# Block attention feeding a token and channel MLP, one core: the first batch in a hand-set order, its values transposed on TensorE, its queries transposed in fp32, and another layout of the DRAM scratch

## Chip, cores and metric

One Trainium2 chip (trn2), one core. Times are device microseconds (us) of whole executions. "Span" is the length of one profiled execution; the named engines are PE (TensorE), DVE (VectorE), ACT (ScalarE), POOL (GpSimd) and SP, which here only issues DMAs. The "granted clock" is the TensorE clock that the throttle let through, as a share of full speed. A run is marked slow when it is over 1.5% above the fastest of the same kernel, and fast otherwise; all comparisons below are of fast runs unless it says otherwise.

## The reference, cut to what matters

```python
# 4 batches, 8 heads, 768 positions of 64, 8 blocks of 96 positions
P = sort_net                                    # 8x8 for each batch and head
for _ in range(5):                              # Sinkhorn
    P = exp(P - max(P)); P = P / rowsum(P); P = P / colsum(P)
k_sorted = einsum('bhij,bhjcd->bhicd', P, k_blocks)     # blocks of keys mixed
v_sorted = einsum('bhij,bhjcd->bhicd', P, v_blocks)     # blocks of values mixed
attn = softmax(q_block @ k_sorted_block.T / 8)          # within each block
x = attn @ v_sorted_block                               # -> (batch, 768, 512)
u = x + lam * (w_tok @ (alpha1 * x + beta1))            # token mixing
out = u + lam * (relu((alpha2 * u + beta2) @ w_ch1) @ w_ch2)   # channel MLP, 512 -> 2048 -> 512
```

## The kernel before: the parts that matter here

Batches are software-pipelined: the attention of batch b is traced ahead of the channel MLP of batch b-1, and a scheduler orders the instructions of each engine. For batch 0 nothing lies before it, so its loads, Sinkhorn, attention and token mixing are a stage of their own. The mixed values come out of the matmul with (head, block) on the partitions, but the attention's product needs the position within a block there. They are regrouped through a scratch tensor in DRAM:

```python
vscr = dram.tile([B, BLK, H * NB, GRP], F16)        # GRP = 66: 64 values, a one for the softmax sum, one of padding
def mix_v(b):
    for n in range(6):
        nc.tensor.matmul(vps, bigV[b], raw[:, n * 512:(n + 1) * 512])
        ...                                          # copied to vA[:, 48, 0:64], vA[:, :, 64:66] = 1
    for th in range(2):                              # write: pieces of 66 float16 = 132 bytes
        nc.sync.dma_start(vscr[b, th * HB:(th + 1) * HB].rearrange("t c d -> c t d"), vA[th * 64:(th + 1) * 64])
    for par in range(2):                             # read: 8.4 KB per partition in one piece
        nc.sync.dma_start(Vs[b % 2][par * HB:(par + 1) * HB],
                          vscr[b].rearrange("(tt par) c d -> par tt c d", par=2)[par])
# ... cut ...
def emit_q(b):      # queries cast to float16 on DVE, 24 transposes on PE, 8 copies on DVE
def prep_wtok():    # w_tok (768x768) turned on PE: 36 transposes of 96 columns, 36 of 32
def prep_affine():  # alpha1*lam, beta1*lam on POOL; six row sums of w_tok on DVE
def prep_w2():      # W2 = W2 * lam on POOL, 16 instructions
def moe_a(b):       # token mixing (tok_ps): u = x + lam*(...), u transposed into a2T
# ... cut ...
mix_v(0); mix_k(0); cast_q(0); emit_q(0); emit_attention(0)
prep_wtok(); prep_affine(); moe_a(0); prep_w2()
for b in range(1, B):
    load_q(b); cast_q(b); ...; mix_v(b); mix_k(b); emit_q(b); emit_attention(b)
    moe_h(b - 1, 0); moe_ch(b - 1, 0); moe_h(b - 1, 1); moe_a(b); moe_ch(b - 1, 1)
```

The softmax here doesn't subtract the row's maximum and nothing guards it: scores larger than these inputs give would overflow.

## Time and profile before

| | before |
|---|---|
| median of the first three runs | 349.29 us (348.66 to 352.27) |
| first product of batch 0 (x_ps) | 70.1 us |
| first token mixing (tok_ps) of batches 0, 1, 2, 3 | 82.0, 145.1, 212.6, 280.4 us |
| PE idle between 47.5 and 70 us | all of it |

From the page's part 2, the span of 348.4 us in 40 equal slices: tenths of busy time for PE, of the granted TensorE clock, and of the 16 DMA engines:

```profile
PE   0358940099777996999959999999599988999995
...
PEclk9975555557999998999998999999899999999999
DMA  7999999931995996019851220597302100201102
```

PE has a hole in slices 7 and 8, the clock stands at 0.5 from slice 4 to 9, and the DMA engines are full from slice 2 to 8. The chain of waits (start, duration, what) says what the hole waited for:

```profile
6.13 25.41 DMA b2col<-in_moe_beta_dram
31.55 0.02 issue
31.56 32.53 DMA vscr<-vA
...
64.53 5.51 DMA Vs_224<-vscr
...
70.08 1.62 PE x_ps L322 x16
...
86.23 17.98 DMA vscr<-vA
...
104.65 5.76 DMA Vs_225<-vscr
```

The write of batch 0's values into the scratch takes 32.5 us of that chain and the read back 5.5; batch 1's write takes 18 and its read 5.8. The page's list of DMA issues (KB each, median us from issue to landing):

```profile
vscr<-vA SPq DMA_DIRECT2D x8, 396.0 KB, 18.1
...
Vs_224<-vscr SPq DMA_DIRECT2D x4, 396.0 KB, 4.8
Vs_225<-vscr SPq DMA_DIRECT2D x4, 396.0 KB, 4.7
```

Each batch has two of these writes, issued together: the same bytes land in 18 us when they are written in 132-byte pieces and in under 5 when they are read in large ones.

Last, two stretches of the first stage (length, then busy time of PE, weight loads, DVE, ACT and POOL with instructions, granted clock, DMA share, GB/s):

```profile
28.00:47.50 19.50, 19.41 (x85) 10.49 (x83) 10.03 (x11) 6.24 (x12) 4.92 (x6) 0.50 1.24 188
47.50:70.00 22.50, 0.00 (x0) 0.00 (x0) 1.12 (x2) 0.75 (x1) 5.59 (x4) 0.50 1.16 167
```

PE works through the transposes of w_tok without a gap and then stops for 22.5 us.

### The profile page before, as it was taken

What the parts mean: (1) busy time and instruction counts of PE and PEld (TensorE: products, weight loads), DVE (VectorE), ACT (ScalarE), POOL (GpSimd) and SP (SyncE); (2) the same over time, 40 slices, a digit from 0 to 9 for tenths busy, and PEclk for the clock granted to TensorE, in tenths of its full rate; (3) what the DMA queues carried; (4) which work ended last, traced back from release to release, by engine and by line L of the source; (5) the groups of instructions that cost most, each with busy time, mean ns of one, the idle gap of its engine ahead of it and who ended that gap; (6) DMA issues with size and microseconds to landing.
All of it is one profiled execution on the core that took longest, in us unless ns stands there. A gap on an engine that the chain in (4) does not pass through costs nothing.

```text
span 348.4 us, 4808 instructions
## 1 busy us (share of the span) xinstructions
PE 281.4 (81%) x1801; PEld 161.7 (46%) x1812; DVE 178.9 (51%) x398; ACT 143.5 (41%) x304; POOL 105.5 (30%) x98
## 2 busy tenths in 40 slices
PE   0358940099777996999959999999599988999995
PEld 0144520084445643554647454546464644454552
DVE  7899300169997822197757603959471046101001
ACT  2252310042597502566446055646450644170620
POOL 6216050006999966001300850031027300000000
PEclk9975555557999998999998999999899999999999
DMA  7999999931995996019851220597302100201102
GB/s 177 243 251 200 183 182 132 185 113 50 66 28 101 215 216 196 2 20 56 50 155 46 78 60 0 34 55 85 106 2 60 31 3 0 81 11 54 38 27 63
DMA packets 41367, 31.85 MB, mean 91 GB/s; under 512 B 27520, under 2 KB 36480, under 8 KB 40960
## 3 DMA queue, kind: packets, MB, share of 16 engines
q1 hardware_dynamic: 35040, 19.88, 39.7%
q0 software_dynamic: 6304, 11.67, 18.1%
q8 instruction: 14, 0.23, 0.3%
q14 instruction: 9, 0.07, 0.1%
HBM read 33.67 MB, written 9.54 MB: 124 GB/s over the span
## 4 chain that ended last, share of the span: by engine, by line
PE 52%; DMA 31%; DVE 10%; SPq 3%; ACT 2%; issue 1%; DVEq 0%
PE ch_ps L451 21%; PE h_ps L439 20%; DMA vscr<-vA 14%; DMA b2col<-in_moe_beta_dram 7%; PE x_ps L322 5%; DMA qf<-in_q_dram 3%; DMA Vs_224<-vscr 3%; DMA Vs_225<-vscr 3%; PE sc_ps L305 3%; PE tok_ps L399 2%; DVE toktmp L404 2%; PE uT_ps L412 1%; DVE qbd_216 L291 1%; DVE ost L456 1%; DVE x_347 L352 1%
## 5 line engine op out<-in xcount | busy, mean ns | idle before, releaser
L443 ACT ACTIVATE hTa<-h_ps 128x384 bf16<-128x384 f32 x96 | 47.0, 492 | 69.0 <-PE h_ps L439 68.4
L439 PEld LDWEIGHTS <-W1p 128*128 128x128 bf16 x512 | 50.3, 101 | 33.3 <-issue 6.5
L451 PE MATMUL ch_ps<-W2p,hTa 128*128 128x512 bf16 x277 | 65.3, 379 | 0.4
L312 ACT ACTIVATE et<-sc_ps 96x384 f16<-96x384 f32 x64 | 27.8, 489 | 46.3 <-PE x_ps L322 34.5
L451 PEld LDWEIGHTS <-hTa 128*128 128x128 bf16 x288 | 27.9, 98 | 32.0
L322 PEld LDWEIGHTS <-et 96*96 96x96 f16 x256 | 19.8, 149 | 36.0 <-DMA Vs_224<-vscr 26.9
L404 DVE TENSOR_TENSOR toktmp<-tok_ps,a1lB 128x512 f32<-128x512 f32 x24 | 16.4, 686 | 35.4 <-PE tok_ps L399 35.3
L322 PE MATMUL x_ps<-Vs_224,et 96*96 96x65 f16 x128 | 11.3, 240 | 26.3 <-DMA Vs_224<-vscr 26.3
L113 DVE CAST qn<-qf 128x768 f16<-128x768 f32 x14 | 9.4, 683 | 35.5 <-DMA qf<-in_q_dram 35.5
L451 PE MATMUL ch_ps<-W2p,hTb 128*128 128x512 bf16 x96 | 24.6, 379 | 0.2
L272 ACT CAST kT<-k_ps 64x256 f16<-64x256 f32 x48 | 17.6, 368 | 16.9 <-PE q_ps L283 11.4
L380 POOL TENSOR_TENSOR W2p<-W2p,lamB 128x512 bf16<-128x512 bf16 x16 | 18.5, 1197 | 12.4 <-DMA W2p<-in_moe_w_ch_dram 12.4
L399 PEld LDWEIGHTS <-w_tokT 128*128 128x128 f16 x144 | 13.9, 98 | 16.2 <-issue 1.7
L270 DVE CAST kT<-k_ps 64x256 f16<-64x256 f32 x48 | 19.9, 415 | 0.8
L329 DVE RECIPROCAL recip<-x_ps 96x4 f32<-96x4 f32 x64 | 9.6, 169 | 20.8 <-PE x_ps L322 20.0
L305 PEld LDWEIGHTS <-kT 128*96 128x96 f16 x128 | 16.0, 148 | 7.6 <-issue 3.1
L443 ACT ACTIVATE hTb<-h_ps 128x384 bf16<-128x384 f32 x32 | 15.7, 490 | 6.0 <-PE h_ps L439 5.5
L439 PE MATMUL h_ps<-a2T_659,W1p 128*128 128x384 bf16 x64 | 14.7, 326 | 0.8 <-DVE a2T_660 L424 0.8
L439 PE MATMUL h_ps<-a2T_660,W1p 128*128 128x384 bf16 x64 | 12.4, 358 | 3.4 <-DVE ost L456 3.4
L451 PEld LDWEIGHTS <-hTb 128*128 128x128 bf16 x96 | 9.4, 98 | 11.3
L439 PE MATMUL h_ps<-a2T_1402,W1p 128*128 128x384 bf16 x64 | 14.4, 337 | 0.0
L322 PE MATMUL x_ps<-Vs_225,et 96*96 96x65 f16 x128 | 9.6, 214 | 5.8 <-DMA Vs_225<-vscr 5.8
(247 smaller groups left out, 462.9 us busy)
## 6 DMA issues: line engine op xcount, KB each, us to landing
qf<-in_q_dram SPq DMA_DIRECT2D x14, 384.0 KB, 5.7
out_dram<-ost SPq DMA_DIRECT2D x24, 192.0 KB, 2.2
vscr<-vA SPq DMA_DIRECT2D x8, 396.0 KB, 18.1
W1p<-in_moe_w_ch_dram POOLq DMA_DIRECT2D x4, 512.0 KB, 21.1
W2p<-in_moe_w_ch_dram POOLq DMA_DIRECT2D x4, 512.0 KB, 23.2
Vs_224<-vscr SPq DMA_DIRECT2D x4, 396.0 KB, 4.8
Vs_225<-vscr SPq DMA_DIRECT2D x4, 396.0 KB, 4.7
out_dram<-ost SPq DMA_DIRECT2D x24, 64.0 KB, 2.0
```

The source lines that it names most:

```text
L270: nc.vector.tensor_copy(dst, src)
L272: nc.scalar.copy(dst, src)
L305: nc.tensor.matmul(sps[:, ii, :, :].rearrange("p a t -> p (a t)"), kT[:, h4 * NB + 2 * g + ii, :], qb[:, 2 * g + ii, :, :].rearrange("p a ...
L312: nc.scalar.activation(et[:], sps[:], AF.Exp, scale=scale)
L322: nc.tensor.matmul(xps[:, ii * 2 + h2, 0:D + 1], ets[g][:, ii, h2, :], Vs[b % NV][:, col, 0:D + 1], start=True, stop=True,)
L329: nc.vector.reciprocal(recip[:], xps[:, :, D])
L380: nc.gpsimd.tensor_tensor(W2p[:, m, :], W2p[:, m, :], lamB[:], ALU.mult)
L399: nc.tensor.matmul(tps[:], w_tokT[:, ks, kt * 128:(kt + 1) * 128], x128[:, ks, :], start=(ks == 0), stop=(ks == NT - 1),)
L404: nc.vector.tensor_tensor(tmp[:], tps[:], a1lB[:], ALU.mult)
L439: nc.tensor.matmul(hps[:], W1p[:, ci, m * 128:(m + 1) * 128], a2T_of[b][hf][:, ci, :], start=(ci == 0), stop=(ci == CT - 1),)
L443: nc.scalar.activation(hT[m], hps[:], AF.Relu)
L451: nc.tensor.matmul(cps[:], hT[m][:, kk * 128:(kk + 1) * 128], W2p[:, m, :], start=(m == 0), stop=(m == HT - 1),)
```

## The change

The intent: keep batch 0's values off the loaded DMA queues, by mixing them the way the keys are mixed and transposing them on PE; transpose its queries straight from fp32, without a cast on DVE; write all of the first stage in the order in which each engine shall run it; and lay out the scratch, which batches 1 to 3 still use, the other way round. The diff, cut to its core:

```diff
+    class Engine:                       # wraps each engine; while fixed, instructions keep their program order
+        fixed = True
+        ...
+                if Engine.fixed:
+                    tc.keep_in_program_order(ins)
-    vscr = dram.tile([B, BLK, H * NB, GRP], F16, name="vscr", tag="vscr")
+    vscr = dram.tile([B, H, NB, BLK, D], F16, name="vscr", tag="vscr")
     # write: now 6 KB per partition in one piece; the ones stay in Vs
-                vscr[b, th * HB:(th + 1) * HB, :, :].rearrange("t c d -> c t d"),
+                vscr[b, :, :, th * HB:(th + 1) * HB, :].rearrange("h i t d -> (h i) t d"),
     # read: now 64 float16 = 128 bytes in one piece
-                Vs[b % NV][par * HB:(par + 1) * HB, :, :],
-                vscr[b].rearrange("(tt par) c d -> par tt c d", par=2)[par],
+                Vs[b % NV][par * HB:(par + 1) * HB, :, 0:D],
+                vscr[b].rearrange("h i (tt par) d -> par tt (h i) d", par=2)[par],
+    def q_first(n):                      # 16 calls, put between the Sinkhorn steps and the mixing of the values
+        for kk in range(3):
+            pe.transpose(qps[:, kk, :], qn_of[0][1][h4][:, h2, 3 * kh + kk, :], ident32[:])   # fp32
+        act.copy(...)
+    def turn_v(b, vT):                   # 32 transposes of 96 columns, 4 copies on DVE
     ...
-        nc.vector.tensor_reduce(rs[:, kt:kt + 1], wt16[:, kt, :], AXX, ALU.add)
+    def prep_rs():                       # the row sums as 36 matmuls with a column of ones
-    mix_v(0)
-    mix_k(0)
-    ...
+    mixing_matrices(0)
+    for g in range(6):
+        vT0 = mix_t(0, 1, share=(4, 4, 3, 2, 1, 1), into=vT0, groups=range(g, g + 1))
+        for n in range(9 + 2 * g, min(11 + 2 * g, 16)):
+            q_first(n)
+    mix_k(0, ps=psb, share=(0,) * 6, groups=range(3))
+    turn_v(0, vT0)
+    mix_k(0, ps=psb, share=(2,) * 6, into=kT_of[0], groups=range(3, 6))
+    ...
+    emit_attention(0, between)           # three of the six parts of w_tok between the scores
+    prep_rs()
+    mix_v(1, alone=True)
+    Engine.fixed = False
     # also: W2 loaded ahead of W1, the first u of batch 0 on ACT instead of POOL, mixing matrices of
     # batches 1 to 3 made when needed, the tail copies split in two, et 6 -> 8 and ost 3 -> 2 buffers
```

## The prediction

> **What bounds the kernel now.** From about 111 us on TensorE does: in the table by 10 us stretches it is busy 9 to 10 us of most. In the chain of waits the first 83 us are: small loads (b2col) to 31.6, one DMA, vscr<-vA, to 64.1, the read back Vs_224 to 70.0, attention to 79, tail copies to 82.9. TensorE is idle from 47.5 to 70.0 and about 5 us more between 14.5 and 28; the first token-mixing matmul (tok_ps) starts at 82.0. The DMA list: batch 0's two vscr writes, in pieces of 132 bytes, land a median of 29 us after issue (18 over all batches), while the weights saturate the 16 engines.
>
> **Removed.** Batch 0's values no longer go to DRAM and back: 38 us of the chain. Its query casts (4 x 0.55 us), 8 copies into qbd (0.96 us each) and the row sums of w_tok (6 x 0.94 us) leave DVE.
>
> **Added.** 32 transposes of mixed values: the like ones of w_tok (96 columns) took about 0.26 us, so 8 us at half clock. 48 fp32 transposes for 24 float16 ones at 0.14 us: estimated 0.2 to 0.45 us each, 10 to 20 us, part of it under the Sinkhorn loop. 36 row-sum matmuls, 4 us. Copies: 16 on ACT (0.5 us by the kT copies), 24 more mixing copies of 0.37 to 0.42 us for six, 4 on DVE of about 1.1 us.
>
> **The new first stage.** Queries land (DMA waits) at 4, 11.6, 16 and 19 us. The hand order puts their copies between the exponentials and ahead of the mixing matmul, so P16 slips from 13.2 to about 15 and mixing starts near 17.5, 3 us later. From there TensorE is dense: mixing 6 us, the other query transposes 5 to 9, values 8, w_tok 17.6, scores 6, products 6, row sums and batch 1's values 7: 55 to 60 us at half clock, about 30 at full. DVE has 29 us then, ACT 25. So tok_ps starts near 75 to 80 if the clock stays at 0.50, near 52 if warm.
>
> **The clock decides.** The granted clock was 0.50 from 22 to 82 us, through 19.5 us of nearly gapless w_tok transposes and 9 us of scores and products[...]. But [...]I expect it warm for a good part: tok_ps near 63, a gain of 19 us.
>
> **Afterwards.** Batch 1's values are written before moe_a(0), in 6 KB pieces, and read in 128-byte ones: about 20 us, against 24 now, hidden. I expect 2 of the 6 us idle between 90 and 111 back. Steady state the same (3.5 us idle per batch for late qf).
>
> 349 - 19 - 2 = 328 us; 8 in 10: 313 to 343. Faster 0.82, same 0.15, slower 0.03.
>
> **Signs.** No wait on vscr or Vs_224 in the first 80 us; first tok_ps at 50 to 78; TensorE over 90% busy from 20 us to there; the rep matmul at 16 to 18; batch 1's first product 20 us after the first tok_ps.
>
> **Wrong if** the clock stays at half throughout (then about 343), fp32 transposes cost over 0.5 us, in-order waits on late queries stall every engine, or batch 1's 128-byte reads take over 25 us.

"Warm for a good part", and with it the 19 us (82 to 63), is the author's estimate, between the two ends given: 75 to 80 at 0.50, 52 at full clock. Its times at full clock are about half of those at 0.50, an estimate from the clock column alone; e13 later measured a pair of 512-column matmuls at 0.60 and 1.06 us, and twelve w_tok transposes at 2.11 and 2.98. The 0.2 to 0.45 us of an fp32 transpose are an estimate too, one and a half to three times the 0.14 measured for float16.

## More of the kernel before

The token mixing's start is a good mark for a stage, since all of a batch's attention lies before it.

The token mixing of each batch, from the timeline of PE (start, duration, instructions):

```profile
82.03 4.31 PE L399 MATMUL tok_ps<-x_347,w_tokT 128*128 128x512 f16 x18
...
145.05 4.05 PE L399 MATMUL tok_ps<-x_923,w_tokT 128*128 128x512 f16 x18
...
212.64 4.05 PE L399 MATMUL tok_ps<-x_1713,w_tokT 128*128 128x512 f16 x18
...
280.38 4.05 PE L399 MATMUL tok_ps<-x_2497,w_tokT 128*128 128x512 f16 x18
```

A batch in the steady part is 67.6 to 67.7 us long. PE's longest wait from 212.6 to 280.4 us (us in total, times, longest) is for the read back:

```profile
PE x_ps L322 <- DMA Vs_225<-vscr: 3.7, 1, 3.7
```

## The result, and the profile after

The changed kernel ran in 326.35 us (median of 4, 325.7 to 327.01), beside 350.4 us for the kernel before in the same rounds: ratio 0.931, 95% interval 0.925 to 0.937. A ratio is the mean of one kernel's fast runs over that of the other's of the same rounds, so it is not quite the ratio of the medians. Repeated on another chip it gave 326.66 us (6 runs) beside 354.8: ratio 0.922. The kernel before moves from chip to chip (348.4 to 354.9 us), the changed one hardly.

The same lines of the changed kernel's page (span 325.0 us, so slices are 8.1 us):

```profile
PE   3466899996699989999999999999999979999995
...
PEclk9976555569999999999999999999999999999999
DMA  7999997049609970039420200493012001202112
```

The hole is gone and the clock column is still at 0.5 for four slices. In the chain of waits no scratch transfer is left in the first stage; what stands there now is:

```profile
2.13 13.36 DMA qf_87<-in_q_dram
15.49 0.14 issue
15.63 0.49 PE qf_ps L66 x3
16.11 0.14 PE rep_ps L66
...
27.77 3.66 PE vt_ps L66 x32
...
33.79 8.83 PE wtok_ps L66 x36
```

The queries' third load holds up PE until 15.6 us and with it the rep matmul, from which the mixing matrices are made, until 16.1, as the prediction said of the in-order queue; the 32 transposes of the values take 3.7 us. The scratch's DMAs (Vs_107 is one of the two buffers that the values are read back into):

```profile
vscr<-vA SPq DMA_DIRECT2D x6, 384.0 KB, 4.3
...
Vs_107<-vscr SPq DMA_DIRECT2D x4, 384.0 KB, 6.9
```

The write fell from 18.1 to 4.3 us; the read, now in the small pieces, rose only from 4.8 to 6.9. (The other buffer's two reads, further down the list, took a median of 5.8.) The token mixing of each batch:

```profile
68.99 5.11 PE L66 MATMUL tok_ps<-x_487,w_tokT 128*128 128x512 f16 x18
...
128.88 1.46 PE L66 MATMUL tok_ps<-x_1055,w_tokT 128*128 128x512 f16 x6
...
193.03 4.05 PE L66 MATMUL tok_ps<-x_1859,w_tokT 128*128 128x512 f16 x18
...
257.19 3.19 PE L66 MATMUL tok_ps<-x_2657,w_tokT 128*128 128x512 f16 x14
```

So of the 23.4 us between the two spans, 13.0 lie before the first token mixing (82.0 against 69.0), 3.1 before the second, 3.4 and 3.6 in the two steady batches (64.15 us each instead of 67.6 and 67.7), and 0.2 after the last. And the stretch that answers to the one of the w_tok transposes before:

```profile
27.70:31.20 3.50, 3.43 (x32) 3.43 (x33) 1.97 (x3) 3.35 (x11) 1.59 (x3) 0.50 1.09 192
31.20:69.00 37.80, 35.31 (x240) 23.83 (x239) 18.07 (x58) 14.90 (x34) 6.61 (x7) 0.50 0.74 129
```

PE is busy 35.3 of 37.8 us, at a granted clock of 0.50 throughout.

### The profile page after: what moved, and what is told of

Read it like the earlier page. It is cut to its first block, busy times and chain, and to the rows that moved or that the text cites. A ratio compares the mean times of both kernels' runs of the same rounds, so it can differ in the third digit from the quotient of the medians.

```text
span 325.0 us, 5050 instructions
## 1 busy us (share of the span) xinstructions
PE 288.8 (89%) x1909; PEld 170.0 (52%) x1922; DVE 173.2 (53%) x403; ACT 157.7 (49%) x338; POOL 98.1 (30%) x95
## 4 chain that ended last, share of the span: by engine, by line
PE 64%; DVE 16%; ACT 8%; DMA 8%; issue 2%; SPq 0%; DVEq 0%; ACTq 0%
PE ch_ps L66 22%; PE h_ps L66 18%; PE wtok_ps L66 5%; PE tok_ps L66 5%; DMA qf_87<-in_q_dram 4%; PE x_ps L66 4%; DVE kT L66 4%; ACT et L66 3%; DVE toktmp L66 3%; PE sc_ps L66 3%; DMA qf<-in_q_dram 2%; ACT kT L66 2%; ACT hTa L66 2%; PE v_ps L66 2%; DMA out_dram<-ost 2%
## 5 line engine op out<-in xcount | busy, mean ns | idle before, releaser
L66 ACT ACTIVATE hTa<-h_ps 128x384 bf16<-128x384 f32 x96 | 46.6, 497 | 64.2 <-PE h_ps L66 63.3
L66 PE MATMUL ch_ps<-W2p,hTa 128*128 128x512 bf16 x275 | 66.9, 379 | 0.4
L66 ACT CAST kT<-k_ps 64x256 f16<-64x256 f32 x63 | 23.2, 369 | 21.0 <-DVE kT L66 19.3
L66 DVE CAST kT<-k_ps 64x256 f16<-64x256 f32 x57 | 23.7, 416 | 1.5 <-PE k_ps L66 0.5
L66 PEld LDWEIGHTS <-w_tokT 128*128 128x128 f16 x180 | 15.3, 101 | 17.2 <-issue 3.3
L66 PEld LDWEIGHTS <-kT 128*96 128x96 f16 x160 | 18.7, 153 | 8.0 <-issue 3.0
L66 POOL TENSOR_TENSOR W2p<-W2p,lamB 128x512 bf16<-128x512 bf16 x16 | 20.2, 1290 | 0.0
L66 PEld LDWEIGHTS <-et 96*96 96x96 f16 x256 | 17.6, 141 | 3.3 <-issue 0.5
L66 PE MATMUL wtok_ps<-ident_72,wt_109 128*96 128x128 f16 x72 | 17.8, 313 | 0.9 <-DVE kT L66 0.9
L66 ACT ACTIVATE hTb<-h_ps 128x384 bf16<-128x384 f32 x32 | 15.6, 491 | 5.4 <-PE h_ps L66 4.7
L66 DVE RECIPROCAL recip<-x_ps 96x4 f32<-96x4 f32 x64 | 9.7, 167 | 14.7 <-PE x_ps L66 14.6
L66 PE MATMUL h_ps<-a2T_813,W1p 128*128 128x384 bf16 x64 | 13.8, 326 | 0.9 <-ACT hTa L66 0.8
L66 PEld LDWEIGHTS <-wt_109 128*96 128x96 f16 x72 | 9.4, 131 | 9.2 <-issue 1.8
L66 PE MATMUL h_ps<-a2T_1537,W1p 128*128 128x384 bf16 x64 | 13.0, 326 | 0.1
L66 PE MATMUL h_ps<-a2T_2341,W1p 128*128 128x384 bf16 x64 | 13.0, 326 | 0.1
```

Of the source, the lines that this page charges most:

```text
L66: ins = getattr(self.eng, name)(*args, **kwargs)
```

## The experiments

Twelve runs, on several chips. Each line's ratio is to the kernel before in the same rounds; "tok" is the first token mixing of batches 0 and 1, "steady" the distance from batch 2's to batch 3's, both from the profiled run. The first two rows are the first measurement. Chips: e1, e2, e6 and e7 share one; the changed kernel again, e3, e8 and e4 another; e5, e9 and e11 a third; e13 had its own. The kernel before was profiled in the first measurement alone, so its stages are known on no other chip, and stages compared with it are good only to a few us where its total differs.

| kernel | median us | before us | ratio (95%) | tok 0 | tok 1 | steady |
|---|---|---|---|---|---|---|
| before | 350.4 | | 1 | 82.0 | 145.1 | 67.7 |
| changed | 326.35 | 350.4 | 0.931 (0.925 to 0.937) | 69.0 | 128.9 | 64.2 |
| e1 layout alone | 333.32 | 354.86 | 0.940 (0.937 to 0.942) | 72.8 | 139.6 | 62.4 |
| e2 changed, old layout (timed rounds all slow) | 343.42 | 354.86 | 0.970 (0.967 to 0.973) | 63.5 | 129.9 | 68.8 |
| e6 changed, values through DRAM | 337.76 | 354.86 | 0.951 (0.949 to 0.954) | 82.0 | 138.5 | 64.3 |
| e7 transposed values alone | 356.35 | 354.86 | 1.004 (1.000 to 1.008) | 61.6 | 146.8 | 69.7 |
| changed, again | 326.66 | 354.8 | 0.922 (0.918 to 0.926) | 68.5 | 127.8 | 64.1 |
| e3 changed, order free | 332.12 | 354.8 | 0.937 (0.932 to 0.941) | 66.2 | 133.7 | 64.1 |
| e8 layout and transposed values | 322.9 | 354.8 | 0.911 (0.907 to 0.914) | 61.7 | 128.5 | 62.4 |
| e4 changed, float16 queries | 325.65 | 354.8 | 0.917 (0.913 to 0.921) | 71.4 | 129.1 | 64.1 |
| e5 changed, w_tok by matmuls | 324.0 | 348.39 | 0.927 (0.921 to 0.932) | 67.3 | 126.2 | 64.1 |
| e9 changed, W2 scaled early | 340.19 | 348.39 | 0.976 (0.972 to 0.980) | 73.7 | 141.4 | 64.1 |
| e11 e8 with W2 early | 324.87 | 348.39 | 0.933 (0.929 to 0.937) | 61.5 | 130.8 | 62.4 |
| e13 changed, filler matmuls | 322.25 | 351.67 | 0.915 (0.910 to 0.920) | 69.5 | 126.3 | 64.1 |

Results were correct in all of them. The theory to start from: the gain is of two kinds, the first stage by the transposed values in a good order (T, O), and the steady batches by the layout alone (L). The rivals: the layout does it all, or the order does.

### e1: the layout alone

```diff
 # kernel before
-    vscr = dram.tile([B, BLK, H * NB, GRP], F16, ...)
+    vscr = dram.tile([B, H, NB, BLK, D], F16, ...)     # and the two DMAs as in the change; ones set once in Vs
```

> The kernel before with one part of the change: the scratch in DRAM is laid out so that the write is in 6 KB pieces and the read back in 128-byte ones. Theory L (layout): the steady batches gain what the changed kernel gained on them after its first token mixing, 3.1 to 3.6 us for each of batches 1 to 3, because the write lands in 4 to 5 us instead of 18 and the read in about 7. In the first stage the write of batch 0 also lands sooner, but the read then competes with the weights, so batch 0's first product moves from 70 to about 60: total 349 - 10 - 9 = about 330. Rival (the steady gain comes from the order or the deeper buffers, not from the layout): the distances between the first token mixings of batches 1, 2 and 3 stay at 67.6 us and the total is 340 or more.

Measured: 0.940, 21.5 us less. The steady batch fell from 67.7 to 62.4 us, more than in the changed kernel. The write landed in 4.4 us (median), the read in 6.3. In the first stage the write of batch 0 took 9.1 us of the chain of waits instead of 32.5, and the read back, now in small pieces under the weights' load, 21.4 instead of 5.5: the first product came at 60.9 us. Batch 1, from the first token mixing to the second, took 66.8 us, against 63.0 in the kernel before, so the 3.1 to 3.6 us expected of each batch were missed both ways. Theory L holds for the steady batches, and one changed access pattern makes most of the whole gain.

### e2: the change with the old layout

```diff
 # changed kernel
-    vscr = dram.tile([B, H, NB, BLK, D], F16, ...)
+    vscr = dram.tile([B, BLK, H * NB, GRP], F16, ...)  # and the two DMAs as in the kernel before
```

> The changed kernel with the old scratch layout for batches 1 to 3 (batch 0 does not use it). Theory L: the first token mixing stays at 69 us, each later batch is 3 to 4 us longer again, total about 336. Rival (order or buffers): total within 2 us of 326.

Measured: 0.970 from the three timed rounds (343.42 to 344.55 us). These three are marked slow, being over 1.5% above the fastest of this kernel, at mean clocks of 0.90 to 0.91; the two runs marked fast are the profiled one, 338.28, and 341.32, which would be 0.953 to 0.962 of 354.86. Either way it is 12 to 18 us above the changed kernel (measured on other chips), and how much of that is the state is not settled. The token mixing of batch 1 is about where the changed kernel has it (129.9), and then the batches are 70.1 and 68.8 us long instead of 64.15. The write landed in 15.1 us (median). This shows the steady gain of the changed kernel to be the layout's. One expectation was missed: the first token mixing did not stay at 69 us but came at 63.5, although batch 0 runs the same instructions on PE. The clock differed: in this execution it stood at 1.00 from 31.8 to 35.1 and from 45.4 to 55.6 us, where the changed kernel's first profile has 0.50. Two lines of PE's timeline show it; the changed kernel's twelve take 2.98 us there:

```profile
48.73 2.11 PE L66 MATMUL wtok_ps<-ident,wt 128*96 128x128 f16 x12
...
52.81 2.11 PE L66 MATMUL wtok_ps<-ident,wt 128*96 128x128 f16 x12
```

So the clock of the first stage is not the same in every execution of the same instructions, and one profile of a stage says little about what raises it.

### e6: the change with batch 0's values through DRAM

```diff
 # changed kernel
-        vT0 = mix_t(0, 1, share=(4, 4, 3, 2, 1, 1), into=vT0, groups=range(g, g + 1))
+        if g == 0:
+            mix_v(0)
-    turn_v(0, vT0)
```

> The changed kernel, in its hand-set order, but batch 0's values regrouped through DRAM in the new layout in place of the transposes on PE. Theory T (the transposes on PE are what frees the first stage): the values' read back is under the weights' load and lands at 45 to 60 us, later than the 32 us at which the transposed values are ready and later than the first product in the changed kernel (48 us), so total 330 to 340. Rival (with the new layout the way through DRAM is short enough to hide behind the w_tok transposes): total within 3 us of 326, or less, since 3.7 us of transposes leave PE.

Measured: 0.951, 337.76 us. The first product waited 17.3 us for the read back and came at 61.6 us, the first token mixing at 82.0. So with the new layout too the way through DRAM is too long for the first stage, and in the fixed order nothing fills the wait. Theory T holds for this order.

### e7: the transposed values alone

```diff
 # kernel before
-    mix_v(0)
+    mix_t0()        # mix_t and turn_v of the change, batch 0 only; copies half on DVE, half on ACT
     mix_k(0)
```

> The kernel before, with only batch 0's values mixed and transposed on PE; everything else and the order as before, old layout for batches 1 to 3. Theory T: the 22.5 us wait for the read back goes, the first token mixing starts at 62 to 70 and the total is about 349 - 14 = 335. If the hand-set order is what matters, the first token mixing stays near 78 and the total near 345.

Measured: 1.004, nothing gained, and both expectations missed. The first product moved from 70.1 to 48.3 us and the first token mixing from 82.0 to 61.6, and yet batch 1's token mixing came at 146.8, later than the 145.1 of the kernel before. (The steady batches were 69.7 us long, 2 us more than in the kernel before's profile; it was slower as a whole on this chip, too.) Its chain of waits says where the 20 us gained by then went:

```profile
61.85 1.31 POOL W2p L381
63.16 1.12 POOL u L395
64.28 1.12 POOL W2p L381
65.40 1.54 POOL u L394
...
88.30 21.40 DMA vscr<-vA
...
110.72 17.16 DMA qf<-in_q_dram
```

First comes a run of POOL's work (scaling W2 and the sums u, taking turns), then batch 1's own write into the scratch, from 88.3 to 109.7 us, and then the loads of the next queries behind it in SP's queue. In the kernel before this write ended at 104.2. The gain turned into two new waits: for POOL, and for the next small-piece write.

### The changed kernel again, on the chip of the next three

> The changed kernel unaltered, on the same chip as the three below, so that they are compared with it directly. 0.925 to 0.937 of the kernel before.

Measured: 0.922, a little better than 0.925 to 0.937. On this chip the kernel before is slower (354.8) and the changed one is not.

### e3: the order left to the scheduler

```diff
 # changed kernel
-        fixed = True
+        fixed = False
```

> The changed kernel with nothing kept in program order: the same instructions, but the scheduler orders the first batch. Theory O (the hand-set order is needed for the transposed values to pay): the order of the later work slips back ahead of it or the batch 1 chain starts late as in the run with the transposes alone, so 8 to 15 us slower than the changed kernel. Rival (the order is worth little, layout and transposes are everything): within 3 us of the changed kernel.

Measured: 0.937, 5.5 us slower than the changed kernel on the same chip; between the two expectations. The first token mixing is earlier (66.2 against 68.5), batch 1's is later (133.7 against 127.8), and from there on the two are equal. For this code the hand-set order is worth 5.5 us, and it earns them in batch 1, not in batch 0.

### e8: the layout and the transposed values, nothing else

```diff
 # e1
-    mix_v(0)
+    mix_t0()        # as in e7
     mix_k(0)
```

> The kernel before with the new layout and batch 0's values transposed on PE, in the scheduler's order, float16 queries. Theory O: the transposes moved the first product forward by 22 us and brought nothing alone, because batch 1 then waited for its own values' 18 us write and for POOL; with the new layout the write is 5 us, so part is kept: 325 to 330 on the scale where the layout alone is 333 and the changed kernel 328 to 330. Rival (hand order needed): no better than the layout alone, ratio 0.94 of the kernel before.

Measured: 0.911, 322.9 us, the best of its chip: 3.8 us faster than the whole change, with intervals that do not overlap. It has the scheduler's order, float16 queries, and the row sums on DVE. With e1 and e7 this makes a square of the two parts: neither 1, transposes alone 1.004, layout alone 0.940, both 0.911. The transposes are worth nothing with the old layout and about 3% with the new one. Batch 1's write says why: it is issued at 87.6 us in e7 and at 87.4 in e8, after the same run of POOL's work, but it has landed only by 109.7 in e7 and already by 92.5 in e8. The rest of the change together costs 1%. Where: the profiled spans differ by 2.7 us (321.1 here, 323.8 for the changed kernel). Batch 1's token mixing comes 0.7 us later here (128.5 against 127.8), the two steady batches are 3.4 us shorter (62.4 us each against 64.1), and the last part is equal.

This puts e3 in its place. In the scheduler's order the whole changed code reaches batch 1's token mixing at 133.7 us, and e8 at 128.5. So the parts of the changed code that e8 does not have cost about 5 us there, and the hand-set order wins them back; it is not a gain over what the scheduler does with the two parts that count.

### e4: float16 queries in the changed kernel

```diff
 # changed kernel, in q_first
+        if n % 4 == 0:
+            dve.tensor_copy(qn[...], qfs[h4])          # 4 casts
-        qps = psb([64, 3, 128], FT, "qf_ps")
+        qps = psb([64, 3, 128], F16, "qf_ps")
-            pe.transpose(qps[:, kk, :], qn_of[0][1][h4][:, h2, 3 * kh + kk, :], ident32[:])
+            pe.transpose(qps[:, kk, :], qn[:, 3 * kh + kk, 2 * h4 + h2, :], ident16[:])
```

> The changed kernel with batch 0's queries cast to float16 on DVE (4 casts of 0.55 us) and the same 48 transposes done in float16. If the fp32 transposes cost PE time on the path, the mixing of the values ends earlier than 27.8 us and the total falls by 1 to 3 us. Rival (fp32 transposes are in the shadow of the late queries and of the copies, and keep the clock up): no change within 2 us, or slower by the casts; if the clock falls to 0.50 before 20 us instead of at 28, the fp32 ones were what kept it up.

Measured: 0.917 against 0.922, with intervals that overlap: no difference shown. The first token mixing came 3 us later here (71.4) and batch 1's 1.3 later. The rate of PE is another matter. Four of the mixing matmuls in the changed kernel, then in e4 (from the timeline of PE; in square brackets the idle time before and what ended it):

```profile
23.66 0.38 PE L66 MATMUL k_ps<-bigP_244,raw_84 128*128 128x128 f16 x4 [1.35 <-ACT qbd_100 L66]
```

```profile
24.05 0.61 PE L66 MATMUL k_ps<-bigP,raw 128*128 128x128 f16 x4
```

In the changed kernel they take 0.38 to 0.39 us from 20.2 to 25.6 us, in e4 0.58 to 0.61 us from 18.6 to 29.1. So with float16 queries PE ran slowly through the stretch in which it ran fast with fp32 ones, although the clock column shows 1.00 for e4 from 18 to 38 us. The rate of the matmuls decides, as the column does not show it here (a like case of the kernel before is in the last section). Whether the fp32 transposes had a part in it is not shown: e4 also has two gaps of 2.2 and 2.6 us in which PE waited for the casts, and the clock differs between executions of one code anyway (e2): in the changed kernel's second profile four such matmuls still take 0.63 us at 23.1 and 0.38 only at 25.1. So the cause was not separated. The totals show that it mattered little.

### e5: w_tok turned by ordinary matmuls

```diff
 # changed kernel, in prep_wtok
-            pst = psb([128, S], F16, "wtok_ps")
-                pe.transpose(pst[0:96, tt * 128:(tt + 1) * 128], wt16[:, tt, ks * 96:(ks + 1) * 96], ident16[:])
+            for hf in range(2):
+                pst = psb([128, 384], FT, "wtok_ps")
+                    pe.matmul(pst[0:96, t3 * 128:(t3 + 1) * 128], wt16[:, tt, ks * 96:(ks + 1) * 96], ident16[:], start=True, stop=True)
```

> The changed kernel with the 72 transposes of w_tok done as ordinary matmuls of the same operands, into two float32 halves (12 copies instead of 6). Theory C ([...]the granted clock was 0.50 from 28 to 69 us in the changed kernel): the clock is 1.0 through most of 34 to 60 us, w_tok takes about 10 us instead of 18, first token mixing near 55 to 60, total 6 to 12 us less than the changed kernel. Rival ([...]as in the scores and products, which are ordinary matmuls and stayed at 0.50): clock 0.50 as before, total within 2 us of the changed kernel, ratio 0.92 to 0.93.

Measured: 324.0 us, 0.927 on a chip where the kernel before is at its fastest, so about the changed kernel. Twelve of the new matmuls take 2.98 us, exactly as long as twelve transposes, and the granted clock of 45 to 66 us is 0.50. It fell from 1.00 to 0.50 at 35.4 us, 2 us into the dense run of these ordinary matmuls. Theory C (it is the transposes as such that keep the clock low) falls: without them the clock was as low. Ordinary matmuls of the same shapes did no better than transposes, and in e2 the transposes ran at the full clock (2.11 us for twelve) among other matmuls.

### e9: W2 scaled ahead of batch 0's attention

```diff
 # changed kernel
     prep_affine()
+    prep_w2()
     prep_wtok(range(3), dve.tensor_copy)
     ...
     moe_a(0)
-    prep_w2()
```

> The changed kernel with the scaling of W2 moved ahead of batch 0's attention on POOL, which idles from 40 to 70 us there and is 91 to 100% busy from 70 to 100. Theory P (POOL holds back the first token mixing: DVE's sums into u take 1.6 us in place of 0.7 while POOL works, and wait for POOL's sums): TensorE's idle time from 70 to 95 us, about 7 us, shrinks to 2 to 4 and the total falls by 3 to 5 us against the changed kernel. Rival (DVE's own work bounds that stretch): within 1 us.

Measured: 0.976, about 14 us above the changed kernel's 326 (measured on other chips), a plain miss. The first token mixing came 5.3 us later than in the changed kernel's second profile (73.7 against 68.5) and batch 1's 13.6 later (141.4 against 127.8). Two lines of its timeline explain the first part, one of POOL and one of DVE:

```profile
35.69 17.92 POOL L66 TENSOR_TENSOR W2p<-W2p,lamB 128x512 bf16<-128x512 bf16 x16
...
43.64 10.12 DVE L66 TENSOR_TENSOR bigP<-mskb,red 128x128 f16<-128x128 f16 x1
```

The DVE product bigP, which reads two operands in SBUF and takes 0.29 us for the other batches, took 10.12 us: it ended at 53.76, just after POOL's sixteenth scaling at 53.61. From its start at 43.64 POOL ran some nine of these scalings, of 1.12 us each, without a gap. So DVE finished nothing until POOL's run was over. That POOL held it fits; by what means is not shown. Behind DVE the attention stopped (PE was busy 4.98 of the 10 us from 50 on).

The larger part, 8.3 us, was lost after the first token mixing. POOL, done with W2, issued the loads of batch 2's values and keys at 82.3 us instead of 95.4, while batch 1's read back from the scratch was under way (chain of waits, then POOL's timeline):

```profile
79.09 25.11 DMA Vs<-vscr
```

```profile
82.31 1.24 POOL L66 DMA_DIRECT2D raw<-in_v_dram  x2
```

That read took 25.1 us, where none of the changed kernel's six took over 10.2 in its second profile, and PE waited 7.0 us for it; the DMA engines were full from 79 to 102 us. That the earlier loads slowed the read fits, but no run separates it. The idle time of POOL was no free time, and an engine that is free sooner starts its transfers sooner.

### e11: the same on e8

```diff
 # e8
-    (W1, then W2 loaded)
+    (W2, then W1 loaded)
+            if b == 0: nc.scalar.activation(u32[kt][:], b1lB[:], AF.Copy, scale=rs[:, kt:kt + 1])
     prep_affine()
+    prep_w2()
     moe_a(0)
-    prep_w2()
```

> The run with the new layout and the transposed values in the scheduler's order, plus W2 loaded ahead of W1 and scaled before the first token mixing, and batch 0's first sums on ACT (both parts of the change or of the run above). There TensorE idled about 11 us between 60 and 90 while POOL was full. Theory P: 6 to 9 us come back, ratio about 0.885 to 0.895 of the kernel before, the best so far. Rival (the scheduler's order of DVE and ACT bounds it): ratio 0.905 to 0.915 as without it.

Measured: 324.87 us, 0.933 on the fast chip: not the 0.885 to 0.895 expected if POOL's late work was what held batch 1 back (theory P), and not clearly better or worse than e8 (322.9 us on another chip). POOL fell from full to 80, 75 and 10% busy in the three stretches from 60 to 90 us, and PE did not gain: it was busy 17.0 of those 30 us, in e8 19.2. Its waits name DVE: 10.8 us for the copies of batch 1's values, which stood behind a cast of queries that waited 7.6 us for its DMA. Another wait took POOL's place.

### e13: filler matmuls

```diff
 # changed kernel
+    def filler(n):          # n matmuls of 128x512 into a PSUM tile that nobody reads
     prep_affine()
+    filler(10)
     prep_wtok(...)          # and filler(2) ahead of each of its six parts
```

> The changed kernel with 22 added matmuls of 512 columns that nobody reads: 10 ahead of the first w_tok transposes and 2 ahead of each sixth of them. Theory C2 ([...]the granted clock is what the prediction's missing part of the first stage is made of): the fillers hold it at 1.0 from about 37 to 65 us, twelve w_tok transposes take 1.5 us in place of 2.98, the first token mixing starts near 60 in spite of the fillers. The total then falls by less than those 8 us, 2 to 6 us, as POOL and DVE bound the stretch from 70 to 95 us. Rival (the clock does not follow such bursts, or falls again within a few us): clock 0.50 in most of 40 to 65 us, first token mixing at 74 to 79, total 4 to 9 us longer.

Measured: 322.25 us, 0.915. Three stretches, with the granted clock:

```profile
33.00:36.20 3.20, 2.55 (x13) 1.19 (x12) 1.47 (x4) 2.07 (x6) 3.19 (x4) 1.00 1.28 239
36.20:49.00 12.80, 12.49 (x91) 7.77 (x89) 3.65 (x11) 3.24 (x9) 7.31 (x7) 1.00 1.22 223
49.00:69.00 20.00, 18.76 (x141) 12.35 (x142) 10.77 (x39) 8.34 (x18) 0.00 (x0) 0.50 0.26 44
```

The clock fell to 0.50 at 28.6 us and was back at 1.00 at 31.9, before the first filler; the mixing matmuls just ahead of the fillers already ran at the fast rate:

```profile
32.63 0.38 PE L66 MATMUL k_ps<-bigP,raw 128*128 128x128 f16 x4 [0.51 <-ACT kT L66]
33.66 2.75 PE L66 MATMUL fill_ps<-raw,ident 128*128 128x512 f16 x12 [0.65 <-DVE kT L66]
```

So the fillers did not raise it. It then stayed up to 49.0 us, through transposes of w_tok, scores, products and three pairs of fillers, and fell. Two more pairs, at 50 and 57 us, did not raise it. The fillers measure the rate themselves: a pair takes 0.60 us up to 45 us and 1.06 afterwards. In e2 and e5, without fillers, the clock rose at 31.8 and 31.9 us too and fell again at 35.1 and 35.4. That the burst held it up would fit, but e2 has a second stretch of 10 us at 1.00 without any filler, and this is one profile: theory C2 is not shown. A full clock saves less than half here: twelve w_tok transposes take 2.11 us at clock 1.00 and 2.98 at 0.50. It is not worth nothing: in e2, where it was up for 13 us of this stage, the first token mixing came 5.5 us earlier than in the changed kernel's first profile. Here the 22 fillers took about 5.6 us themselves (from their starts to those of what follows), and the first token mixing came at 69.5 us, no earlier than without them. The total is on a chip of its own; whether the 4 us to the changed kernel's 326 are the fillers', or the chip's, was not tested. In e13 and e5 the executions with the highest mean clock were the shortest: 320.2 us at 0.973 and 324.6 at 0.947 in e13, 320.45 at 0.956 and 323.5 to 324.4 at 0.926 to 0.950 in e5. Among the changed kernel's own, at 0.925 to 0.951, no such order shows.

## Why the prediction was right, point by point

- **Total.** Predicted 328 us, range 313 to 343; measured 326.35. That it came so close is luck: two terms were off by 6 and 8 us in opposite directions. In the profiled execution the clock was at half for most of the first stage, and for half throughout the prediction's own text gives about 343.
- **What bounded the kernel before** (the scratch transfers): right for the first stage. PE's wait for Vs_224 is gone in the changed kernel. But e7 shows that this reading was not enough: with that wait taken away alone, the time did not move, since the next batch's write was right behind it.
- **Queries' in-order waits**: predicted mixing from 17.5 us, P16 at 15, the rep matmul at 16 to 18. Measured 17.1, 13.8 and 16.1 (P16 is the result of the Sinkhorn steps).
- **First stage, predicted gain 19, measured 13.0.** The step that was off is the clock: "I expect it warm for a good part". PE was fast only from about 20 to 26 us (by its k_ps matmuls) and at 0.50 from 28 to 69. (That is one execution: the second profile has 34.0 to 37.5 us at 1.00, and e2, at 1.00 for 13 us more, has the first token mixing at 63.5, where the prediction put it for a clock warm for a good part.) In the kernel before the clock rose at 82.4 us, 0.4 us after the first token-mixing matmul; what raised it is not shown. Two of the costs were lower than estimated and made up for some of it: the values' transposes 3.7 us instead of 8, and row sums with batch 1's values about 5 instead of 7 (62.9 to 67.8 us). "About 30 us at full clock" was also too low: e13 measures 2.11 against 2.98 us for the largest part, so full clock saves 29% there. In the kernel before the clock cost little: on the third chip the two runs with a mean clock of 0.99 took 346.5 and 347.5 us, the seven other fast ones, at 0.88 to 0.90, 347.6 to 350.9, with a median of 348.4 (two at 0.97 took 353.2 and 353.7 and are marked slow).
- **Afterwards, predicted gain 2, measured 10.4.** The step that was off: "Steady state the same", with "about 20 us, against 24 now" for the scratch. Moving the small pieces from the write to the read made it 4.3 + 6.9 = 11 us instead of 18.1 + 4.8 = 23. Of these 12 us, e1 and e2 show some 5 to be on the path of each steady batch: alone, the new layout takes 5.2 to 5.3 us off it (67.6 and 67.7 to 62.4; against e7, which has the old layout on the same chip, 7.3), and the old one put back into the changed kernel adds 4.6 to 5.9. The 3.5 us of idle time per batch that the prediction put down to late queries had this same cause: in the kernel before, the longest wait of PE in the two steady batches is 3.6 and 3.7 us, for the read back itself, and SP issues the queries' loads behind the scratch's. After each of these waits the clock stood at 0.50 for some 3.4 us (181.4 to 184.8 and 249.7 to 253.1), and eight x_ps matmuls took 0.82 us there against 0.54 at 186.6. In e8's first steady batch it stayed at 1.00. So a part of the gain beyond the wait itself may be the clock's; it was not separated.
- **Signs.** Right: no scratch wait in the first 80 us, first token mixing between 50 and 78. Wrong: PE was only 57% busy from 20 to 30 us, held by copies on ACT (its k_ps matmuls waited 2.6 us for the queries' copies), and 90 to 100% in the stretches of 10 us from there. Batch 1's first product came 26.6 us after the first token mixing instead of 20; the values were there, and the scores waited for DVE's copies into qbd, the chain's pieces from 89.2 to 97.7 us.

What stays open: why the steady batch of the changed code is 1.7 us longer than with the layout alone (64.1 against 62.4). In a steady batch of the changed kernel PE waits 1.7 us for ACT (0.9 for copies of the keys, 0.8 for casts of u), where in e8 it waits 0.4 us for DVE's; which of the small parts (mixing matrices made in the loop, split tail copies, other buffer counts) brings that was not tried. Also open is what exactly the clock follows.

The recommendation from these runs is e8, two parts of the change in the kernel before: 322.9 us, faster than both.

## What to carry to other kernels

When a layout must be turned through DRAM, look at which side of the transfer has the small pieces before building anything around the wait: here one changed access pattern made 6% and the best version needed no hand-set order at all. The small-piece read was not always short: a median of 6.9 us in the changed kernel, but 21.4 beside the weights in e1 and 25.1 in e9. Removing the longest wait pays only if what stands right behind it is short: look one batch further along the chain, and test two parts alone and together. Idle time of POOL is not always free: in e9 a DVE product of two SBUF operands took 10.12 us beside POOL's scalings, in the changed kernel 0.29. Before laying a clock's rise to a change, look whether it came first, and at more than one execution.

## Hardware figures that the traces show

- Scratch in DRAM: 792 KB (two DMAs of 396, issued together) written in 132-byte pieces took 18.1 us, and 768 KB (two of 384) read in 128-byte pieces 6.9 us (medians). The pieces differ in size and alignment too (132 bytes apart against 128), a write in 128-byte pieces was not tried, and the reason for the difference was not tested.
- DVE beside POOL: in e9 a DVE operation that takes 0.29 us in the changed kernel lasted 10.12 us, through a run of POOL instructions of 1.12 us each.
- Transposes and the clock: in e5 ordinary matmuls of the same shapes took the same 2.98 us for twelve as the transposes did, at the same 0.50; in e13 the clock stayed at 1.00 for 17 us through a mixture of transposes and matmuls, and in e2 for 10 us without added matmuls.
- What the full clock saves: for weights of 96 and 32 columns with 128 moved, twelve took 2.11 us at the full clock and 2.98 at half (e13).
- fp32 transposes of 128x64 took 0.14 to 0.23 us each in the changed kernel: twelve in 2.74 us at 10 us, and six in 0.82 us at 20 us, where four k_ps matmuls took 0.39 instead of the 0.58 to 0.63 of 17 to 19 us.
- Early in two traces the clock column read 1.00 while matmuls ran at about half rate (e4 above is one): in the kernel before, six matmuls of 512 columns at 14.6 us took 2.74 us under such a 1.00, where twelve of the same size took 2.75 us at 119 us.
